# A retention and gated-MLP kernel on one core: the table that sets the order of its first two batches is written anew

## The chip, the cores and the metric

The kernel runs on one core of one Trainium2 chip. The metric is the device time of one execution in microseconds (us), the median of three runs. TensorE (PE) multiplies, VectorE (DVE), ScalarE (ACT) and GpSimd (POOL) work on its results and prepare its operands, and SyncE (SP) issues every DMA. Each engine runs its own instructions in the order in which the program lists them, and waits on semaphores for what other engines or DMAs produce.

## The reference

There are 8 batches of 576 tokens. Retention over 8 heads of 64 columns gives x; a gated MLP follows, in which one half of the hidden columns is normalised and multiplied over tokens by a matrix that all batches share.

```python
scores = scale * np.matmul(q, k.transpose(0, 1, 3, 2))
Dmat = np.where(rel >= 0, gamma[:, None, None] ** rel[None, :, :], 0.0)
x = np.matmul(scores * Dmat, v)             # 8 x 576 x (8 * 64)
h = np.maximum(x @ w_in, 0.0)               # 512 -> 1024
u, v = h[..., :512], h[..., 512:]
v_n = (v - mean(v)) / np.sqrt(var(v) + 1e-06)
v_s = np.einsum('ts,bsd->btd', w_spatial, v_n) + b_spatial[None, :, None]
out = (u * v_s) @ w_out                     # 512 -> 512
```

## The kernel before

Retention goes in chunks of 128 tokens, four to a batch, and a tail of 64. Of a chunk, `load` fetches three or one blocks (qk, kn, vv); PE makes the scores (`r<-qk`) and the state's update (`r<-vv,kn`), which needs kn scaled; DVE masks the scores (`at`); ACT or DVE adds the update to the decayed state (`sh` after 64 tokens, `st` after 128); and a burst of PE multiplies the queries with the state and the masked scores with the values (`r<-qsc,sh`, `r<-qsc,st`, `r<-at,vv`). ACT and DVE take the burst's result out in two parts of a number (`slot`, high and low). These products are 64x64 and come in blocks of 16 instructions, each of which the trace shows as two.

The MLP's products have 128 rows and 288, 256 or 512 columns. A number stands as a rounded high part and a low part, so that each product is three. The weights come as 64-bit numbers and are taken apart on the chip: `weight` makes of one block the steps `f` or `lent_vn` (sign), `m<-raw` or `m<-lent_slot` (ACT), two shifts on DVE, the high part (`win`, `wout`, on ACT) and the low part. `split_chain` turns the gated product into high and low parts in `slot`, which `f_chain`, the last product of batch 0, reads (`m<-slot,wout`).

The order of all this is written out. `ORDER` is a text of 714 steps for batches 0 and 1 and the first steps of batch 2; `STEADY` repeats for batches 2 to 5, and `LAST` ends the kernel. `run` takes the names one after the other and lets the chain of that name do its next step; `next(chain)` issues the step's instructions, and every instruction is kept in this order on its engine. So one table sets five queues at once. A name is a kind and its numbers: `d.1.0` issues the loads of batch 1, chunk 0, one a step; `D.2.1` those of a weight block (2 is `w_out`, 0 is `w_u`); `w.0.1.vp` takes one apart; `g`, `p` and `b` are scores, state and burst of a chunk; `k` scales kn; `v` is the normalised half; `V`, `G` and `P` are the spatial product, the gate and the split of batch 0; `F.0.0.3` is its last product, half 0, block 3. `z.N.1` is one idle multiplication of 512 columns (`m<-wsp`) that nobody reads: 43 of them stand in the table. `BANKS` gives each accumulation its PSUM bank, in the order of use.

```python
    def run(order, b=0):
        ...
            chain = chains.get(name)
            if chain is None:
                chain = chains[name] = makers[head](*rest)
            next(chain)
```

The buffer `raw` holds two weight blocks side by side; `fetch(2, 1)`, which is `D.2.1`, writes the half that `D.0.1` filled before and that the second shift of `w.0.1` reads.

Of the kernel before, what the change touches and what calls it, by code (L numbers as in the profile page):

```python
# [40 lines left out]


ORDER = """
    d.0.0 m z.41.1 z.34.1 d.0.0 c.a d.0.0 k.0.0.v q.0.0.p z.33.1 z.37.1 z.1.1 z.12.1 z.18.1 z.25.1 z.15.1 z.10.1
# [4 lines left out]
    w.1.2.pp b.0.1 p.0.1.aa w.1.2.pp b.0.1 b.0.1 z.20.1 v.0.0 z.27.1 z.17.1 z.39.1 z.22.1 w.1.1.vp b.0.1 p.0.1.aa
    b.0.1 v.0.1 w.1.2.pp w.1.2.pp k.0.2.a g.0.2 p.0.2.aa w.1.2.pp w.1.1.vp w.1.3.vp w.1.2.pp v.0.0 z.42.1 v.0.1  # L50
    z.36.1 v.0.0 v.0.0 v.0.1 v.0.1 D.0.2 D.0.1 d.0.3 w.0.2.pp q.0.2.p p.0.1.aa w.0.2.pp p.0.2.aa g.0.2 p.0.2.aa
    p.0.2.aa w.0.2.pp w.0.1.vp w.0.1.vp w.0.1.vp w.0.2.pp w.0.1.vp T.0 S d.1.0 S d.1.0 d.1.0 c.t D.0.0 S d.1.1
    d.1.1 d.1.1 t.0.p q.0.3.p k.1.0.p k.0.3.a b.0.2 g.0.3 b.0.2 v.0.0 t.0.p b.0.2 b.0.2 p.0.3.ap p.0.2.aa b.0.2
    v.0.0 b.0.2 p.0.3.ap v.0.1 v.0.0 v.0.0 t.0.p g.0.3 v.0.1 z.26.1 z.29.1 z.11.1 z.5.1 v.0.2 v.0.2 v.0.2 z.9.1
    v.0.2 z.23.1 z.24.1 z.14.1 v.0.0 p.0.3.ap p.0.3.ap w.0.0.vp b.0.3 s.2.p v.0.1 b.0.3 g.1.0 v.0.0 w.0.0.vp v.0.2
    g.1.0 w.0.0.vp b.0.3 b.0.3 p.1.0.pp g.1.1 e.0.v e.0.v e.0.v w.0.0.vp v.0.1 v.0.4 v.0.4 v.0.4 z.16.1 z.35.1
    s.1.p b.0.3 w.0.2.pp p.1.0.pp w.0.0.vp v.0.1 b.0.3 v.0.3 v.0.3 v.0.4 v.0.3 v.0.3 q.1.0.p s.2.p k.1.1.p s.1.p
    p.1.0.pp w.0.0.vp d.1.2 S S v.0.2 w.0.1.vp v.0.2 v.0.2 s.3.p v.0.2 v.0.4 v.0.1 v.0.2 U.0 U.1 b.1.0 v.0.4 s.5.p
    v.0.4 v.0.3 s.0.p p.1.0.pp v.0.4 p.1.1.pp v.0.4 b.1.0 U.1 v.0.3 U.0 v.0.3 s.4.p g.1.1 v.0.3 v.0.3 v.0.4 v.0.3
    v.0.4 b.1.0 b.1.0 D.2.1 d.1.2 T.1 D.2.0 D.2.2 d.1.2 s.3.p w.0.2.pp q.1.1.p d.1.3 d.1.3 d.1.3 D.0.3 s.0.p G.1.2  # L60
    q.1.2.p p.1.0.pp s.5.p s.4.p v.0.4 v.0.4 p.1.1.pp p.1.1.pp p.1.1.pp w.0.1.vp k.1.2.p p.1.1.pp w.0.3.pv V.0.0
    V.0.0 V.0.0 V.0.0 V.0.3 V.0.0 V.1.0 b.1.0 V.0.0 b.1.0 V.0.3 w.2.1.vp w.2.1.vp V.1.0 w.2.1.vp V.1.2 V.0.2
    w.2.1.vp w.2.0.vv V.1.2 w.2.0.vv b.1.1 p.1.2.pa w.2.1.vp b.1.1 w.0.3.pv w.2.0.vv G.1.2 w.2.0.vv w.0.3.pv
    w.0.3.pv g.1.2 b.1.1 b.1.1 w.0.3.pv V.0.2 V.1.1 G.0.2 v.1.0 D.2.3 d.2.0 d.2.0 A.0.5.v A.0.0.v w.0.3.pv g.1.2
    p.1.2.pa w.2.2.vv G.0.3 V.1.1 w.2.0.vv p.1.2.pa p.1.2.pa G.0.2 q.1.3.p A.0.1.p k.1.3.p w.2.2.vv G.0.3 A.0.2.v
    A.0.6.v t.1.p V.0.1 G.0.1 p.1.2.pa V.0.1 b.1.1 b.1.1 w.2.0.vv v.1.0 A.0.9.v A.0.12.v w.2.2.vv p.1.3.pp b.1.2
    b.1.2 A.0.3 A.0.7 A.0.13.v A.0.14 P.0.1.p w.2.2.vv G.0.1 g.1.3 t.1.p b.1.2 b.1.2 v.1.0 V.1.3 v.1.0 G.1.3 v.1.1
    v.1.1 v.1.1 v.1.1 A.0.15.v p.1.3.pp w.2.3.vp p.1.3.pp w.2.1.vp d.2.1 d.2.0 d.2.1 b.1.2 t.1.p g.1.3 b.1.2 V.1.3
    A.1.5.p v.1.0 w.2.3.vp G.1.3 w.2.3.vp w.2.3.vp p.1.3.pp k.2.0.v v.1.0 b.1.3 b.1.3 p.2.0.vp b.1.3 g.2.0 b.1.3
    G.1.1 e.1.v P.0.0.p v.1.0 e.1.v e.1.v v.1.0 G.1.1 P.0.0.p P.0.1.p v.1.4 v.1.4 v.1.4 y.1.2.0 v.1.4 p.2.0.vp  # L70
    v.1.1 v.1.1 w.2.3.vp v.1.0 v.1.1 v.1.0 b.1.3 w.2.2.vv y.1.2.0 v.1.4 A.0.10 P.1.0.v y.1.1.0 y.1.1.0 A.0.4.v
    A.1.1.v w.2.2.vv v.1.1 v.1.1 v.1.1 g.2.0 p.2.0.vp y.1.0.0 F.0.0.0 y.1.0.0 F.0.0.0 P.1.1.v A.0.11.v A.0.8.v
    P.1.1.v b.1.3 v.1.4 F.0.0.2 v.1.2 v.1.2 F.0.0.1 v.1.2 v.1.2 v.1.4 w.2.3.vp F.0.0.1 F.0.0.2 v.1.2 A.1.0.v
    p.2.0.vp p.2.0.vp A.1.2.p A.1.3 P.1.0.v F.0.1.0 F.0.0.0 F.0.0.1 A.1.6.v A.1.9.v v.1.2 A.1.12.p v.1.4 A.1.13.v
    A.1.7 F.0.1.0 F.0.1.1 v.1.2 F.0.1.1 F.0.0.3 F.0.0.3 v.1.4 v.1.4 v.1.4 v.1.4 v.1.2 v.1.4 q.2.0.v F.0.0.3 F.0.1.0
    F.0.1.1 F.0.0.2 F.0.1.3 F.0.1.3 A.1.14 v.1.3 v.1.3 v.1.3 v.1.3 F.0.1.2 g.2.1 b.2.0 v.1.3 v.1.3 v.1.3 F.0.1.2
    v.1.3 b.2.0 v.1.3 y.1.3.1 y.1.2.1 y.1.3.1 k.2.1.a y.1.2.1 y.1.1.1 A.2.1.v A.1.4.p A.2.5.v A.1.15.p A.2.0.p
    A.2.2.v A.2.6.v v.1.3 A.2.9.v A.1.8.v A.2.12.v y.1.1.1 A.2.7 v.1.2 b.2.0 b.2.0 T.2 d.2.1 p.2.1.vv d.2.2 d.2.2
    d.2.2 F.0.1.3 y.1.3.0 g.2.1 v.1.2 X.1.1.2 X.1.1.2 A.2.3 A.2.10 A.1.10 b.2.0 X.1.0.0 X.1.0.1 y.1.0.1 q.2.1.v
    t.2.v A.2.11.v p.2.1.vv y.1.3.0 A.2.8.v b.2.1 b.2.1 p.2.1.vv p.2.1.vv k.2.2.v p.2.1.vv A.1.11.v X.1.0.1 X.1.0.0  # L80
    A.2.13.v A.2.14 y.1.0.1 A.2.15.v g.2.2 b.2.1 p.2.2.vv b.2.1 d.2.3 d.2.3 d.2.3 X.1.1.3 X.1.1.0 X.1.1.1 g.2.2
    A.2.4.v p.2.2.vv X.1.1.3 p.2.2.vv p.2.2.vv X.1.1.0 b.2.1 Y.1.3.p Y.1.1.v k.2.3.v Y.1.1.v X.1.1.1 Z.1.5.vv
    X.1.0.2 q.2.2.p b.2.2 b.2.2 Y.1.3.p Z.1.7.vv p.2.2.vv X.1.0.2 Z.1.6.vv p.2.3.vp t.2.v b.2.2 g.2.3 b.2.2
    W.1.2.0.A X.1.0.3 W.1.2.1.A Z.1.7.vv b.2.2 Z.1.6.vv W.1.2.0.A Z.1.5.vv p.2.3.vp q.2.3.v d.3.0 d.3.0 F.0.1.2
    t.2.v p.2.3.vp g.2.3 p.2.3.vp Z.1.6.vv Z.1.7.vv X.1.0.3 b.2.3 b.2.3 Y.1.2.v Z.1.5.vv k.3.0.v Y.1.2.v g.3.0
    b.2.3 b.2.3 e.2.p W.1.2.1.A W.1.2.0.A Z.1.4.vv e.2.p W.1.2.0.A Z.1.4.vv e.2.p R.2.1.v W.1.2.0.C W.1.2.0.B
    Z.1.4.vv W.1.2.0.C W.1.2.0.A W.1.2.1.A W.1.2.1.B W.1.2.0.A b.2.3 W.1.2.1.A R.2.3.v W.1.2.1.A W.1.2.1.C
    W.1.2.1.A R.2.2.p R.2.1.v K.2.5.vp W.1.2.0.B W.1.2.0.C d.3.1 d.3.0 W.1.2.0.B R.2.3.v W.1.2.1.C W.1.2.1.E
# [962 lines left out]
```

## Time and profile before

| | |
|---|---|
| median of 3 runs | 503.67 us (502.77, 503.67, 505.89) |
| the profiled execution's own time | 504.22 us |
| its span, first to last instruction | 502.4 us |
| PE busy | 495.2 us of the span |
| DVE, ACT, POOL busy | 391.3, 259.4, 154.1 us |
| moved by DMA | 55.53 MB |

The time of an execution is its span and 1.8 us around it. Busy PE is not PE at its peak, since multiplications overlap: what counts is when the next one begins.

### The profile page before, as it was taken

Reading aid. Unit: us, or ns where it says so; the run is one execution under the profiler, and the core shown is the slowest. Engines: PE = TensorE matmul, PEld = TensorE weight load, DVE = VectorE, ACT = ScalarE, POOL = GpSimd, SP = SyncE. Lnnn points to the kernel's source line nnn. Section 1 sums busy time; section 2 is a strip of 40 time slices with the busy share of each in tenths; the row PEclk is TensorE's granted clock in tenths of the full one; section 3 lists DMA queues with packets and bytes.
Section 4 is the critical chain, followed back from the end, with each engine's and each line's share of the span. In section 5 each row is a group of like instructions: output and inputs, shape, how many; then the busy total and the mean of one; then the engine's idle time right before and its main releaser. Section 6 shows DMA issues by size and latency. Waiting matters only on the chain.

```text
span 502.4 us, 17010 instructions
## 1 busy us (share of the span) xinstructions
PE 495.2 (99%) x7335; PEld 472.8 (94%) x7335; DVE 391.3 (78%) x869; ACT 259.4 (52%) x587; POOL 154.1 (31%) x133
## 2 busy tenths in 40 slices
...
GB/s 303 418 271 316 77 146 24 24 102 97 98 142 164 162 86 2 87 208 123 50 10 156 136 168 0 44 168 165 91 2 64 225 94 3 1 48 48 2 1 94
DMA packets 26429, 55.53 MB, mean 111 GB/s; under 512 B 2929, under 2 KB 11249, under 8 KB 26098
## 3 DMA queue, kind: packets, MB, share of 16 engines
...
q14 instruction: 18, 0.15, 0.1%
...
## 4 chain that ended last, share of the span: by engine, by line
PE 94%; DVE 2%; ACT 1%; DMA 1%; issue 1%; POOL 0%; SPq 0%; ACTq 0%
PE m L203 79%; PE r L203 14%; DMA vv<-in_qkv 1%; ACT places L203 0%; DVE x L203 0%; POOL x L203 0%; DVE u L203 0%; DVE lent_vn L203 0%; DVE m L203 0%; ACT slot L203 0%; SPq L203 0%; DVE o L203 0%; DVE xt L203 0%; ACT xt L203 0%; DVE places L203 0%
## 5 line engine op out<-in xcount | busy, mean ns | idle before, releaser
L203 PE MATMUL m<-wsp,vn 128*128 128x288 f32 x768 | 112.7, 296 | 0.0
L203 PEld LDWEIGHTS m<-wsp,vn 128*128 128x128 f32 x768 | 105.0, 188 | 0.6
L203 DVE TENSOR_TENSOR u<-m,u 128x288 f32<-128x288 f32 (+1 forms) x132 | 57.1, 438 | 23.2 <-PE m L203 11.9
L203 ACT COPY u<-m 128x288 f32<-128x288 f32 (+1 forms) x92 | 34.8, 386 | 40.8 <-PE m L203 33.4
L203 PE MATMUL m<-slot,win 128*128 128x288 f32 x336 | 49.8, 296 | 0.0
L203 PEld LDWEIGHTS m<-slot,win 128*128 128x128 f32 x336 | 46.3, 188 | 0.9 <-ACT vn L203 0.2
L203 ACT CAST slot<-u 128x576 fp32r<-128x576 f32 x32 | 21.5, 675 | 45.3 <-DVE u L203 44.6
L203 DVE SCALAR_TENSOR_TENSOR u<-u,m 128x288 f32<-128x288 f32 x48 | 21.3, 451 | 26.6 <-PE m L203 26.4
L203 PE MATMUL m<-slot,wout 128*128 128x288 f32 x264 | 37.5, 294 | 0.0
L203 PEld LDWEIGHTS m<-slot,wout 128*128 128x128 f32 x264 | 36.0, 188 | 0.2
L203 PE MATMUL m<-win,slot 128*128 128x512 f32 (+1 forms) x168 | 36.2, 349 | 0.0
L203 ACT CAST places<-u 128x576 fp32r<-128x576 f32 x21 | 14.2, 675 | 39.0 <-DVE u L203 39.0
L203 POOL TENSOR_TENSOR dec<-st,fixed_terms 128x256 f32<-128x256 f32 x16 | 14.3, 895 | 64.6 <-DVE st L203 64.6
L203 POOL TENSOR_TENSOR qk<-qk,fixed_terms 128x512 f32<-128x512 f32 (+1 forms) x16 | 21.9, 1369 | 35.3 <-PE r L203 29.9
L203 PEld LDWEIGHTS m<-win,slot 128*128 128x128 f32 x168 | 26.7, 188 | 4.2 <-DVE slot L203 0.5
L203 PE MATMUL m<-quarter,slot 128*128 128x256 f32 x216 | 28.9, 281 | 0.1
L203 POOL TENSOR_TENSOR slot<-u,slot 128x576 fp32r<-128x576 f32 x7 | 10.0, 1436 | 59.5 <-ACT slot L203 53.9
L203 PEld LDWEIGHTS m<-quarter,slot 128*128 128x128 f32 x216 | 27.1, 188 | 0.7 <-ACT u L203 0.3
L203 PE MATMUL m<-wtl,vt 128*128 128x288 f32 (+1 forms) x128 | 27.2, 295 | 0.0
L203 PE MATMUL m<-places,wout 128*128 128x288 f32 x168 | 26.3, 297 | 0.0
L203 PE MATMUL m<-slot,part 128*128 128x288 f32 x168 | 25.3, 298 | 0.0
L203 DVE TENSOR_TENSOR at<-r,fixed_terms 128x512 f32<-128x512 f32 x32 | 21.9, 683 | 3.9 <-PE r L203 2.0
...
## 6 DMA issues: line engine op xcount, KB each, us to landing
qk<-in_qkv SPq DMA_DIRECT2D x30, 512.0 KB, 4.0
...
lent_slot<-in_w_v SPq DMA_DIRECT2D x4, 512.0 KB, 8.4
raw<-in_w_u SPq DMA_DIRECT2D x4, 512.0 KB, 10.8
```

The costliest lines, as they stand in the source:

```text
L203: ins = op(*args, **kw)
```

## The change

`ORDER` and `BANKS` are written anew. The 714 steps are the same ones, each as often as before, the 43 idle multiplications among them, on the same engines; only their order and the banks differ. `STEADY`, `LAST` and every function are unchanged.

```diff
 ORDER = """
-    d.0.0 m z.41.1 z.34.1 d.0.0 c.a d.0.0 k.0.0.v q.0.0.p z.33.1 z.37.1 z.1.1 z.12.1 z.18.1 z.25.1 z.15.1 z.10.1
-    z.3.1 z.4.1 z.28.1 g.0.0 p.0.0.va z.31.1 z.7.1 p.0.0.va b.0.0 z.8.1 D.1.0 D.1.3 g.0.0 w.1.0.vp p.0.0.va
+    c.a d.0.0 d.0.0 k.0.0.v q.0.0.p m d.0.0 z.26.1 z.13.1 z.29.1 z.2.1 z.21.1 z.34.1 z.32.1 z.4.1 z.14.1 z.16.1
+    z.28.1 z.22.1 g.0.0 p.0.0.va z.40.1 z.0.1 z.39.1 p.0.0.va b.0.0 D.1.0 p.0.0.va p.0.0.va g.0.0 w.1.0.vp w.1.0.vp
...
```

The first place is the start. On DVE before, the mask of chunk 0 (`at_161`) stands ahead of the first state, and the low part of the burst's result (`slot_189`) ahead of the shifts for the first weight blocks; `sh`, which the burst of chunk 1 needs, is the last row here.

```order
L203 TENSOR_TENSOR kn_95<-kn_95,fixed_terms 128x512
L203 TENSOR_TENSOR at_161<-r_91,fixed_terms 128x512
L203 TENSOR_SCALAR lent_vn_92<-lent_slot_93 128x512
L203 TENSOR_TENSOR dec_79<-sh,fixed_terms 128x256
L203 TENSOR_TENSOR st_76<-r_91,dec_79 128x256
...
L203 TENSOR_TENSOR slot_189<-r_90,slot_189 128x2x4x64
L203 SCALAR_TENSOR_TENSOR m_87<-m_87,lent_vn_92 128x512
L203 SCALAR_TENSOR_TENSOR lent_vn_92<-lent_slot_93,m_87 128x512
L203 SCALAR_TENSOR_TENSOR m_86<-m_86,lent_vn_92 128x512
L203 SCALAR_TENSOR_TENSOR lent_vn_92<-lent_slot_93,m_86 128x512
L203 TENSOR_TENSOR sh<-r_91,dec_78 128x256
```

DVE now, the same stretch.

```order
L203 TENSOR_TENSOR kn_96<-kn_96,fixed_terms 128x512
L203 TENSOR_TENSOR dec_79<-sh,fixed_terms 128x256
L203 TENSOR_TENSOR st_76<-r_91,dec_79 128x256
L203 TENSOR_TENSOR at_161<-r_91,fixed_terms 128x512
L203 TENSOR_SCALAR lent_vn_92<-lent_slot_93 128x512 x2
L203 SCALAR_TENSOR_TENSOR m_89<-m_89,lent_vn_92 128x512
L203 SCALAR_TENSOR_TENSOR lent_vn_92<-lent_slot_93,m_89 128x512
L203 SCALAR_TENSOR_TENSOR m_87<-m_87,lent_vn_92 128x512
L203 SCALAR_TENSOR_TENSOR lent_vn_92<-lent_slot_93,m_87 128x512
L203 TENSOR_TENSOR slot_197<-r_90,slot_197 128x2x4x64
L203 TENSOR_SCALAR lent_vn_92<-lent_slot_93 128x512
L203 TENSOR_TENSOR sh<-r_91,dec_78 128x256
```

The state of chunk 0 now comes ahead of its mask, and `sh` of chunk 1 stands behind one more instruction, the sign step of the third weight block (`TENSOR_SCALAR lent_vn`), which before stood right behind it.

ACT a little later, before: the rows that stand ahead of the scaling of chunk 2's kn (`u<-u`, eight instructions), which the update of chunk 2 on PE needs.

```order
L203 ACTIVATE dec_79<-sh,fixed_terms 128x64 x4
L203 ACTIVATE m_86<-lent_slot_93 128x512
L203 CAST win_66<-lent_vn_92 128x512
L203 CAST slot_189<-r_90 128x2x4x64
L203 ACTIVATE u<-u,fixed_terms 128x64 x8
```

ACT now.

```order
L203 ACTIVATE dec_79<-sh,fixed_terms 128x64 x4
L203 CAST win_66<-lent_vn_92 128x512
L203 CAST slot_197<-r_90 128x2x4x64
L203 ACTIVATE m_87<-lent_slot_93 128x512
L203 ACTIVATE u<-u,fixed_terms 128x64 x8
```

A step of the fourth weight block (`m<-lent_slot`) moved from ahead of the two casts to behind them.

The second place is SP's queue between the first loads and batch 1. Before, qk of batch 1, chunk 0 (`qk_94`) is issued behind one row of the spatial matrix (`in_w_sp`), and its kn and vv (`kn_95`, `vv_417`) soon after; the first `w_out` block comes later, after the rows shown.

```order
L203 DMA tail<-in_tails 128x768
L203 DMA lent_slot_93<-in_w_sp 128x576
L203 DMA qk_94<-in_qkv 128x1024
L203 DMA lent_slot_93<-in_w_sp 128x576
L203 DMA kn_95<-in_qkv 128x512
L203 DMA vv_417<-in_qkv 128x512
L203 DMA amt<-in_tmask 128x256
L203 DMA raw<-in_w_u 128x512
```

SP now, from the same tail on.

```order
L203 DMA tail<-in_tails 128x768
L203 DMA qk_199<-in_qkv 128x1024
L203 DMA kn_200<-in_qkv 128x512
L203 DMA raw<-in_w_out 128x512
L203 DMA raw<-in_w_u 128x512
L203 DMA amt<-in_tmask 128x256
L203 DMA qk_95<-in_qkv 128x1024
L203 DMA lent_slot_93<-in_w_sp 128x576
L203 DMA kn_96<-in_qkv 128x512
L203 DMA vv_432<-in_qkv 128x512
```

Two blocks of chunk 1 (`qk_199`, `kn_200`) and two weight blocks, the first of which is `D.2.1`, now go ahead of the blocks of chunk 0 (`qk_95`, `kn_96`, `vv_432`).

The third place is the first product of batch 0 with `w_out`, some 80 us into the program. On PE before, the burst of batch 1's last chunk (`att,tail` is its end) is followed by products of `win` with `slot` and with `xt`; the first `m<-slot,wout` comes 40 rows later.

```order
L203 MATMUL r_90<-at_266,vv_417 64x64 x16
L203 MATMUL r_90<-att,tail 64x64 x8
L203 MATMUL m_88<-slot_189,win_66 128x288 x2
L203 MATMUL m_88<-slot_189,win_67 128x288
...
L203 MATMUL m_87<-win_66,xt 128x512
L203 MATMUL m_87<-win_67,xt 128x512
```

PE now.

```order
L203 MATMUL r_90<-at_261,vv_432 64x64 x16
L203 MATMUL r_90<-att,tail 64x64 x8
L203 MATMUL r_91<-vv_201,kn_96 64x64 x16
L203 MATMUL m_86<-slot_197,wout_1095 128x288 x2
L203 MATMUL m_86<-slot_197,wout_1098 128x288
...
L203 MATMUL m_89<-slot_197,win_66 128x288 x2
L203 MATMUL m_89<-slot_197,win_67 128x288
```

`F.0.0.3`, the last of its four blocks before, now is the first, and stands right behind the burst and one update. The two instructions of POOL that make the low parts for it (`slot<-u,slot`, two steps `P`) keep their place among POOL's rows.

## Rows read from the trace of the kernel before

**Rows 1.** Windows: length, busy PE, PEld, DVE, ACT, POOL, PEclk, DMA, GB/s.
```profile
8.00:21.30 13.30, 12.30 (x297) 9.19 (x297) 10.34 (x19) 9.85 (x29) 7.71 (x7) 1.00 1.03 419
21.30:45.30 24.00, 23.94 (x428) 19.94 (x426) 19.78 (x47) 22.05 (x59) 17.66 (x16) 1.00 0.86 317
45.30:160.00 114.70, 114.70 (x1732) 109.52 (x1733) 94.14 (x185) 60.06 (x136) 44.84 (x38) 1.00 0.33 103
160.00:176.90 16.90, 16.50 (x419) 15.80 (x422) 14.10 (x40) 10.05 (x25) 7.91 (x8) 1.00 0.46 148
```

**Rows 2.** Timeline of PE to 45: start, length, what, [idle before, releaser].
```profile
8.05 0.69 PE L203 MATMUL r<-vv,kn 64*64 64x64 f32 x32 [0.33 <-DMA vv<-in_qkv]
...
15.62 0.24 PE L203 MATMUL r<-qsc,sh 64*64 64x64 f32 x1 [0.57 <-DVE sh L203]
...
16.46 0.27 PE L203 MATMUL r<-qsc,st 64*64 64x64 f32 x1 [0.38 <-ACT r L203]
...
17.32 0.50 PE L203 MATMUL m<-wsp 128*128 128x512 f32 x1
...
18.36 1.09 PE L203 MATMUL m<-wsp 128*128 128x512 f32 x4
19.28 0.96 PE L203 MATMUL m<-win,slot 128*128 128x512 f32 x3
20.17 1.16 PE L203 MATMUL r<-u 64*64 64x64 f32 x64
21.26 0.96 PE L203 MATMUL m<-win,slot 128*128 128x512 f32 x3
```

**Rows 3.** Timeline of PE, 168.8 to 171.
```profile
170.01 0.44 PE L203 MATMUL r<-vv,kn 64*64 64x64 f32 x10 [0.40 <-issue]
```

**Rows 4.** Timeline of DVE, 8 to 36.
```profile
15.05 0.42 DVE L203 TENSOR_TENSOR sh<-r,dec 128x256 f32<-128x256 f32 x1
15.39 0.42 DVE L203 TENSOR_SCALAR lent_vn<-lent_slot 128x512 int32<-128x512 int32 x1
15.72 0.68 DVE L203 TENSOR_TENSOR at<-r,fixed_terms 128x512 f32<-128x512 f32 x1
...
17.10 0.69 DVE L203 SCALAR_TENSOR_TENSOR lent_vn<-lent_slot,m 128x512 int32<-128x512 int32 x1
...
26.80 1.28 DVE L203 SCALAR_TENSOR_TENSOR f<-raw,m 128x512 int32<-128x512 int32 x2
```

**Rows 5.** Timeline of ACT, 8 to 36.
```profile
17.32 0.61 ACT L203 ACTIVATE m<-lent_slot 128x512 f32<-128x512 f32 x1
17.88 0.60 ACT L203 CAST win<-lent_vn 128x512 fp32r<-128x512 f32 x1
18.39 0.57 ACT L203 CAST slot<-r 128x512 fp32r<-128x512 f32 x1
18.87 2.02 ACT L203 ACTIVATE u<-u,fixed_terms 128x64 f32<-128x64 f32 x8
```

**Rows 6.** DMA issues of window 15.6 to 16.0: count, KB, us to landing.
```profile
qk<-in_qkv SPq DMA_DIRECT2D x1, 512.0 KB, 10.9
```

**Rows 7.** Timeline of POOL, 0 to 46.
```profile
27.98 1.04 POOL L203 TENSOR_TENSOR kn<-kn,fixed_terms 128x512 f32<-128x512 f32 x1
```

**Rows 8.** Timeline of PE, 33.3 to 37.
```profile
35.41 0.68 PE L203 MATMUL r<-vv,kn 64*64 64x64 f32 x32
35.88 0.68 PE L203 MATMUL r<-qk 64*64 64x64 f32 x32
```

**Rows 9.** Timeline of POOL, 70 to 110.
```profile
83.83 2.88 POOL L203 TENSOR_TENSOR slot<-u,slot 128x576 fp32r<-128x576 f32 x2 [5.53 <-DVE slot L203]
```

**Rows 10.** Timeline of PE, 62 to 112.
```profile
80.07 0.27 PE L203 MATMUL r<-qsc,sh 64*64 64x64 f32 x1
...
82.61 1.86 PE L203 MATMUL m<-slot,win 128*128 128x288 f32 x12
...
90.90 3.33 PE L203 MATMUL m<-slot,wout 128*128 128x288 f32 x24
```

More of the change, by code (lines that the diff above doesn't have):

```diff
@@ L49 @@
[L49 to L88, printed above, removed]
@@ L89 @@
-    W.1.2.0.B W.1.2.0.E q.3.0.p K.2.7.pv R.2.2.p W.1.2.1.B K.2.6.vp W.1.2.0.E K.2.4.vp W.1.2.0.B W.1.2.1.C d.3.1
-    W.1.2.0.B d.3.1 W.1.2.1.B W.1.2.1.B p.3.0.pv K.2.5.vp K.2.7.pv K.2.7.pv K.2.6.vp p.3.0.pv p.3.0.pv W.1.2.1.E
-    W.1.2.1.B K.2.6.vp W.1.2.0.E W.1.2.1.E p.3.0.pv W.1.2.1.B K.2.4.vp g.3.0 p.3.0.pv K.2.5.vp K.2.4.vp
+    c.a d.0.0 d.0.0 k.0.0.v q.0.0.p m d.0.0 z.26.1 z.13.1 z.29.1 z.2.1 z.21.1 z.34.1 z.32.1 z.4.1 z.14.1 z.16.1
+    z.28.1 z.22.1 g.0.0 p.0.0.va z.40.1 z.0.1 z.39.1 p.0.0.va b.0.0 D.1.0 p.0.0.va p.0.0.va g.0.0 w.1.0.vp w.1.0.vp
@@ new lines @@
+    b.0.0 z.15.1 D.1.3 b.0.0 b.0.0 w.1.3.vp w.1.0.vp w.1.3.vp z.31.1 z.12.1 z.10.1 z.19.1 z.17.1 z.27.1 b.0.0 d.0.1
+    d.0.1 d.0.1 k.0.1.p q.0.1.p g.0.1 p.0.1.aa z.37.1 z.1.1 z.38.1 z.20.1 z.33.1 z.7.1 z.30.1 w.1.0.vp w.1.3.vp
+    w.1.3.vp b.0.0 D.1.1 D.1.2 w.1.1.vp d.0.2 p.0.0.va p.0.1.aa g.0.1 b.0.1 w.1.3.vp w.1.0.vp w.1.1.vp w.1.1.vp
+    w.1.1.vp b.0.1 p.0.1.aa w.1.0.vp w.1.2.pp w.1.1.vp z.36.1 z.8.1 b.0.1 b.0.1 b.0.1 p.0.1.aa b.0.1 z.18.1 v.0.0
+    z.6.1 v.0.1 w.1.2.pp w.1.2.pp w.1.2.pp k.0.2.a g.0.2 p.0.2.aa w.1.1.vp w.1.3.vp w.1.2.pp w.1.2.pp q.0.2.p
@@ new lines @@
+    z.41.1 z.11.1 z.35.1 v.0.0 v.0.1 v.0.1 v.0.0 v.0.1 v.0.0 D.0.1 d.0.3 D.0.2 S S T.0 w.0.2.pp p.0.1.aa w.0.1.vp
+    w.0.1.vp p.0.2.aa w.0.1.vp g.0.2 p.0.2.aa p.0.2.aa w.0.1.vp w.0.2.pp k.0.3.a d.1.1 d.1.1 D.2.1 D.0.0 c.t d.1.0
+    S d.1.0 d.1.0 b.0.2 p.0.3.ap g.0.3 s.1.p b.0.2 q.0.3.p k.1.1.p t.0.p s.1.p t.0.p b.0.2 b.0.2 q.1.0.p k.1.0.p
+    v.0.0 p.0.2.aa b.0.2 w.0.2.pp w.0.2.pp v.0.0 g.0.3 z.25.1 z.24.1 z.9.1 z.3.1 z.23.1 b.0.2 v.0.1 v.0.0 v.0.0
+    p.0.3.ap v.0.2 v.0.2 v.0.2 z.42.1 z.5.1 v.0.2 t.0.p v.0.1 p.0.3.ap v.0.0 p.0.3.ap s.0.p w.0.2.pp v.0.0 b.0.3
@@ new lines @@
+    w.0.0.vp b.0.3 g.1.0 g.1.0 b.0.3 b.0.3 g.1.1 p.1.0.pp w.0.0.vp s.2.p w.0.0.vp e.0.v e.0.v e.0.v w.0.0.vp v.0.4
+    v.0.4 v.0.4 v.0.4 v.0.2 v.0.1 v.0.1 b.0.3 w.0.0.vp p.1.0.pp b.0.3 v.0.3 v.0.3 v.0.3 v.0.3 v.0.1 w.0.1.vp v.0.2
+    v.0.1 v.0.2 v.0.4 v.0.2 v.0.2 v.0.4 w.0.0.vp v.0.2 U.0 U.1 b.1.0 s.0.p p.1.0.pp s.2.p q.1.1.p p.1.0.pp p.1.0.pp
+    w.0.2.pp T.1 S d.1.1 S v.0.4 v.0.3 v.0.3 v.0.4 p.1.1.pp s.3.p U.0 s.4.p s.3.p D.2.2 d.1.2 d.1.3 v.0.3 b.1.0
+    b.1.0 b.1.0 v.0.4 U.1 s.5.p v.0.3 p.1.1.pp v.0.4 v.0.3 s.4.p s.5.p w.0.1.vp G.1.2 V.0.0 v.0.3 b.1.0 V.0.0 V.0.0
@@ new lines @@
+    v.0.4 v.0.4 v.0.4 V.0.3 V.0.0 V.0.3 V.1.2 V.1.2 g.1.1 b.1.0 G.1.2 V.0.0 V.1.0 D.2.0 w.2.0.vv w.2.0.vv V.1.0
+    w.2.0.vv V.0.0 D.0.3 d.1.2 d.1.3 k.1.3.p p.1.1.pp q.1.2.p p.1.1.pp d.1.3 d.1.2 w.2.0.vv w.2.1.vp k.1.2.p
+    p.1.1.pp w.0.3.pv V.0.2 b.1.1 b.1.1 g.1.2 b.1.1 b.1.1 p.1.2.pa w.0.3.pv V.0.2 V.0.1 G.0.1 b.1.1 b.1.1 w.0.3.pv
+    g.1.2 w.0.3.pv V.1.1 V.0.1 w.2.1.vp w.0.3.pv w.0.3.pv G.0.1 w.2.1.vp w.2.1.vp A.0.0.v p.1.2.pa t.1.p p.1.2.pa
+    q.1.3.p A.0.1.p v.1.1 v.1.1 v.1.1 w.2.0.vv w.2.1.vp w.2.1.vp w.2.0.vv D.2.3 w.2.3.vp w.2.3.vp v.1.1 v.1.0 v.1.1
```

31 lines of the change are left out of this document (27 added, 4 removed).

## The prediction

> **What bounds the kernel now.** I read the windows first, since the change touches one stretch: the table's steps run from the start to some 177 us, and everything behind them keeps its order. In that stretch PE is the engine that is never free. From 45.3 to 160 us it is busy for 114.70 of 114.70 us, from 21.3 to 45.3 for 23.94 of 24.00, while DVE, the next, has 94.14 of 114.70 [rows 1]. A new order can't shorten PE's work, for the list of steps is the same; it can only take away waits of PE or add some. So the second reading is PE's timeline at the start, the only place where it waits. DMA fills that place: its share is 1.03 from 8.0 to 21.3 us, at 419 GB/s [rows 1].
>
> PE's waits there are four. The first update of a state begins at 8.05, when vv lands. The burst of chunk 1 waits 0.57 us for `sh` from DVE and, half way, 0.38 for ACT [rows 2]. Behind them come idle multiplications, from 17.32 on, that wait for nothing and cost 0.23 us each (four of them take PE from 18.36 to 19.28) [rows 2]. That is the hidden reserve: the 43 idle multiplications are time on PE whether it has a wait to fill or not. Last, one gap of 0.40 us in the middle of a block of updates near 170 us, for which no semaphore is named [rows 3]. The three gaps together are 1.35 us; with them gone the kernel would be 0.3% faster. Anything below about 1% (5 us) can hardly be told from no change here, as the runs before lie 3 us apart.
>
> **The start, worked out.** Until the data land, nothing differs: the terms, qk, kn and vv of chunk 0 are loaded in another order, but vv is the fourth in both, so the first update stays at 8.05 [rows 2], and 12 idle multiplications in place of 13 ahead of it cost or save nothing.
>
> Then the burst of chunk 1. On DVE the same instructions stand ahead of `sh` as before and one more, the sign step of the third weight block, which ran right behind it. The two change places, so `sh` comes one spacing later: 15.39 in place of 15.05, a shift of 0.34 [rows 4]; if that weight block lands late, some tenths more. I take 0.44. The burst's first half goes from 15.62 to 16.06. Its second half had waited for ACT until 16.46; now two idle multiplications lie between the halves, and the masked scores come from DVE behind `sh` as before (`at`, 15.72 before, 16.16 now, 0.68 long) [rows 4], so the values can start at 16.9 to 17.1. The burst is over, and the next idle multiplication starts, at about 17.8, against 17.32 [rows 2]: 0.48 later. But the changed order has by then spent 31 of the 43 idle multiplications, the old one 26 (I counted the z steps on PE's row). Five of them, 1.15 us, have moved into time in which PE would have waited. Balance here: 0.48 - 1.15 = -0.67 us.
>
> The next wait takes most of it back. The update of chunk 2 (the second half of the 64 `r<-u` at 20.17 [rows 2]) needs kn scaled by eight ACT instructions that ran from 18.87 to 20.89 [rows 5]. Before, ACT did one weight step at 17.32 ahead of the two casts; now it does it behind them, right ahead of the scaling, and the first cast needs a DVE shift that ran from 17.10 to 17.79 [rows 4]. On DVE the same instructions stand ahead of that shift in both orders, only turned among themselves, so I move its end by no more than 0.1, to 17.87. ACT's chain is then: cast 17.9, second cast 18.4, weight step 18.9, scaling from 19.5 (spacings of 0.51, 0.48 and 0.56 between such rows [rows 5]), end 21.5 to 21.6. The update's last part ends at 21.75, and the next product starts at 21.9 in place of 21.26 [rows 2]: 0.64 later. Up to here 33 idle multiplications are spent against 31, which gives back 0.46. Balance: **+0.2 us**, and it replaces the -0.67, as both are counted from the start. The bounds: if the weight step doesn't delay the scaling (0.6), the balance is -0.4; if the third block lands so late that `sh` loses 0.5 more, +0.7.
>
> **The loads of batch 1.** Before, qk of chunk 0 of batch 1 was issued at about 15.7 and landed 10.9 us later, at 26.6 [rows 6], and kn was scaled at 27.98 for an update at 35.41 [rows 7, 8]: a cover of over 6 us. Now two blocks of 512 KB and two small ones go ahead on SP's queue, and the first (`D.2.1`) waits until DVE has done the second shift of the block that lies in its place. That shift is the second of the pair that began at 26.80 and ended at 28.08 before [rows 4]; in the new order it stands ahead of the pair's other half, so I put it between 25.9 and 28.1. From there to kn's landing lie 512, 512, 128, 512, 288 and 256 KB, 2.26 MB, which is 5.4 us at 419 GB/s [rows 1]. DMA is full until about 27.9 with what goes ahead, so kn lands at about 33.3, is scaled by 34.4 (1.04 [rows 7]), and the update, which now stands behind the scores of the next chunk (0.47, from 35.41 to 35.88 [rows 8]) and two more idle multiplications, comes at 36.5. Cost: nothing, with 2 us of cover left. If the shift ends at 28.1 rather than 25.9 and nothing else fills DMA until then, those 2.2 us come on top, and PE waits 0.2, with tenths of DMA's spread 0.5 us. I take 0.
>
> **The rest.** From 45 to 160 us PE has no wait to lose [rows 1], so a new order can only cost there. The place with the least cover that I found is the first product with `w_out`. Before, POOL made the low parts for it from 83.83 to 86.71 [rows 9], and PE came to it at 90.90 [rows 10], 4.2 us later. Now it stands where PE is at about 82.7: right behind the burst and one update, which ended at 82.61 [rows 10]. ACT's second cast for it stands behind the copy of a product that PE ends before the 12 products and the burst ahead of `F.0.0.3`: 12 times 0.14 (24 take 3.33), and 80.07 to 82.61 [rows 10], 4.2 us together. In them must fit three ACT instructions of 0.6 [rows 5] and one of POOL, half of 2.88 [rows 9]: 3.2 us. The cover is 1.0 us. Cost: 0, and from there one for one. All other moves I take together at nothing, since PE's row between 90 and 160 us has the same blocks in nearly the same lengths, and DVE, ACT and POOL have the same work with 18% and more to spare [rows 1].
>
> **The gap near 170 us.** I leave its 0.40 us in. The profile shows that PE stood still inside a block of 32 updates with 10 of them left, and names no releaser [rows 3]; that it was a load of instructions is likely and not shown. If it is gone, -0.4.
>
> The Trainium skill (Runtime: NRT & Kernel Launch, section Instruction fetch mechanics) says that each engine fetches its instructions itself in blocks of 256 ahead of use, and that the cost of a block's edge is mostly hidden. By that rule an order made for late loads of instructions would gain nothing anywhere, and the 0.40 us would stay. The trace agrees as far as 45 to 160 us go, where PE has no idle time, and the row near 170 us speaks against it.
>
> **The sum.** 504.22 of the profiled execution + 0.2 + 0 + 0 = 504.4. That execution was 0.55 over the median, so the median comes to 503.67 + 0.2 = **503.9**, which is no change. Its own range is 502.7 to 505.2: the start's bounds (-0.4, +0.7), the loads' 0.5 and the spread of single runs.
>
> **Rivals.** *Slower: `F.0.0.3` comes too early.* If DVE or ACT is behind at 78 us by more than the 1.0 us of cover, PE waits for the low parts. The upper bound is that POOL ends them when it did before, at 86.71: PE then waits 86.7 - 82.7 = 4.0 us. Time 505 to 507.9; the middle is 506. For it speaks that DVE is the busiest engine behind PE there, against it that POOL's own row is unchanged and it waited 5.53 us for DVE's part before [rows 9], so POOL has room. It decides from the moment that the second cast begins later than about 80.7.
>
> *Faster: the waits go and don't come back.* The scaling isn't delayed, the five idle multiplications stay hidden, and the gap near 170 us goes: -0.67 - 0.4 - 0.3 (tenths that PE waits for single rows between 21.3 and 36; 0.06 of them are in [rows 1]) = -1.4, which gives 502.3. More isn't there: the idle time of PE from 8 to 177 us is 1.46 us [rows 1].
>
> *The change doesn't do what it says.* If loads of instructions never held an engine in this stretch but for that gap, the order is simply another one of the same worth. That gives the forecast's time again, 503.9, and can't be told from it by the time.
>
> **Chances.** Forecast with the third rival 0.64; slower through an early `F.0.0.3` or a like wait 0.20; faster 0.16. A gain over 1% would need 5 us and PE has 1.46 to give: 0.02. A loss over 1% needs the slow rival at its end and a second wait beside it: 0.07. Within 1%: 0.91. The range for 8 in 10 goes from 501.6 to 507.2: from a little below the fast rival's 502.3 to most of the slow one's.
>
> **What would show it.** In the profile after, DVE's `sh` near 15.5; the idle multiplication behind the burst of chunk 1 near 17.8; ACT's eight scalings starting near 19.5 and the next `m<-win,slot` near 21.9; qk of batch 1 landing at 32 rather than 26.6 with no wait of PE at 36; `m<-slot,wout` first at 82.8 without idle time ahead of it; and a PE that is busy all through 45 to 160 us. I am wrong if PE waits there for DVE, ACT or POOL, or if the first update is no longer at 8.05.

## The result, and the profile after

The changed kernel takes 507.25 us (median of 9 runs) against 503.62 for the kernel before (9 runs): a ratio of means of 1.0069, interval 1.0051 to 1.0087. It is 3.6 us slower, under 1%, at the very end of the range (507.2); the forecast of 503.9 missed what costs it. One of the nine, the execution that was profiled first, ran at a granted clock of 0.56 from about 8 us to its end (790 us); the ratio leaves it out, and the median without it is 507.15. The lines below are from two later executions of the same kernel: *first* (508.39 us, its own time) and *second* (506.51).

The windows of the table's stretch, first execution, which answer to [rows 1] (length, busy PE, PEld, DVE, ACT, POOL, PEclk, DMA, GB/s):

```profile
8.00:21.30 13.30, 13.29 (x280) 9.40 (x272) 10.77 (x20) 10.15 (x29) 7.69 (x6) 1.00 1.02 417
21.30:45.30 24.00, 23.52 (x423) 19.66 (x420) 19.39 (x47) 22.09 (x59) 16.68 (x15) 1.00 0.80 281
45.30:160.00 114.70, 112.59 (x1702) 107.57 (x1702) 87.57 (x179) 57.83 (x131) 42.09 (x35) 0.99 0.32 102
160.00:176.90 16.90, 16.90 (x340) 16.32 (x340) 14.59 (x36) 9.06 (x21) 11.36 (x11) 1.00 0.57 188
```

The start has become better: PE's idle time between 8 and 21.3 us went from 1.00 to 0.01. But PE now waits 0.48 us in the second row, and at its end the two kernels are level: PE has begun 763 multiplications by 45.20 us before and 763 by 45.28 now. The damage is in the third row, where PE had been busy for 114.70 us and now is for 112.59, at a clock of 0.99. All 2.1 us are one wait, in none of the three places that were shown ahead of the prediction. It is what the timeline of all engines from 47 to 55 us shows (first execution; start, length, what, idle time before and releaser):

```profile
48.13 2.94 POOL L203 TENSOR_TENSOR wtl<-lent_slot,wtl 1x576 fp32r<-1x576 f32 x2
...
48.63 2.94 PE L203 MATMUL m<-wsp,vn 128*128 128x288 f32 x21
...
51.11 0.59 ACT L203 CAST slot<-r 128x512 fp32r<-128x512 f32 x1 [2.83 <-POOL wtl L203]
51.59 1.26 ACT L203 ACTIVATE vt<-m,sm 64x512 fp32r<-64x512 f32 x2
52.88 0.74 DVE L203 SCALAR_TENSOR_TENSOR vt<-m,sm,vt 64x512 fp32r<-64x512 f32 x1 [3.82 <-ACT vt L203]
...
53.68 0.53 PE L203 MATMUL m<-wtl,vt 128*128 128x288 f32 x2 [2.10 <-DVE vt L203]
```

The same stretch of the kernel before, in lines not shown yet:

```profile
48.48 2.92 POOL L203 TENSOR_TENSOR wtl<-lent_slot,wtl 64x576 fp32r<-64x576 f32 x2
48.55 1.26 ACT L203 ACTIVATE vt<-m,sm 64x512 fp32r<-64x512 f32 x2
...
49.84 0.75 DVE L203 SCALAR_TENSOR_TENSOR vt<-m,sm,vt 64x512 fp32r<-64x512 f32 x1 [0.42 <-ACT vt L203]
...
51.44 0.59 ACT L203 CAST slot<-r 128x512 fp32r<-128x512 f32 x1 [1.64 <-POOL wtl L203]
...
51.65 0.70 PE L203 MATMUL m<-wtl,vt 128*128 128x288 f32 x4
```

ACT's copy of batch 1's first burst (`slot<-r`, the fifth step of `b.1.0`) waits for POOL in both, and POOL is no later now (it ends its rows `wtl` at 51.07, before at 51.40). The copy writes `slot` of batch 1, the buffer in which the rows of the spatial matrix lie until POOL has made the last low parts of `wtl`. Before, that wait of 1.64 us held nobody: the two instructions that make `vt` stood ahead of the copy. In the new table the last three steps of `v.0.4` stand behind it, so `vt` is held until POOL is done, DVE's part follows ACT's, and the spatial product on PE, which needs `vt` for its last two multiplications, stands still.

Behind the wait the clock fell. The windows of the first execution, and of the second, in the same columns:

```profile
53.70:55.00 1.30, 1.30 (x9) 1.30 (x10) 1.24 (x2) 0.40 (x1) 1.30 (x2) 0.96 0.05 19
55.00:58.40 3.40, 3.40 (x16) 3.40 (x16) 0.32 (x1) 0.72 (x2) 2.39 (x3) 0.51 0.00 0
58.40:62.00 3.60, 3.60 (x31) 3.44 (x34) 2.31 (x7) 0.32 (x1) 0.01 (x1) 1.00 0.00 0
```
```profile
53.60:55.00 1.40, 1.36 (x10) 1.36 (x11) 1.29 (x2) 0.40 (x1) 1.23 (x2) 1.00 0.04 15
55.00:58.40 3.40, 3.40 (x28) 3.40 (x27) 1.04 (x2) 1.04 (x2) 2.64 (x3) 1.00 0.00 0
```

After a pause of 2.10 us PE ran at 0.51 (1.2 GHz) for the 3.4 us of the second row and did 16 multiplications there; after one of 2.06 us, in another execution of the same program, it stayed at full speed and did 28. The two executions were level ahead of the pause (48.63 and 48.64); the part of the spatial product that begins at 59.96 in the first begins at 58.39 in the second, 1.57 us sooner. The pause is in both; the fall of the clock is not.

### The profile page after: what moved, and what is told of

It reads as the page before. It is cut to its first block, busy times and chain, and to the rows that moved or that the text cites. A ratio compares the mean times of both kernels' runs of the same rounds, so it can differ in the third digit from the quotient of the medians.

```text
span 788.8 us, 17019 instructions
## 1 busy us (share of the span) xinstructions
PE 783.9 (99%) x7335; PEld 700.1 (89%) x7335; DVE 392.1 (50%) x869; ACT 259.6 (33%) x587; POOL 148.2 (19%) x133
## 4 chain that ended last, share of the span: by engine, by line
PE 99%; DVE 0%; issue 0%; ACT 0%
PE m L203 85%; PE r L203 14%; DVE wsp L203 0%; DVE o L203 0%; ACT r L203 0%; DVE warm L203 0%; DVE eps L203 0%
## 5 line engine op out<-in xcount | busy, mean ns | idle before, releaser
L203 PE MATMUL m<-wsp,vn 128*128 128x288 f32 x768 | 177.9, 406 | 0.0
L203 PEld LDWEIGHTS m<-wsp,vn 128*128 128x128 f32 x768 | 153.4, 222 | 13.1
L203 PE MATMUL m<-slot,win 128*128 128x288 f32 x336 | 77.9, 402 | 0.0
L203 PEld LDWEIGHTS m<-slot,win 128*128 128x128 f32 x336 | 66.7, 216 | 7.4 <-issue 1.6
L203 PE MATMUL m<-slot,wout 128*128 128x288 f32 x264 | 59.7, 391 | 0.0
L203 PE MATMUL m<-win,slot 128*128 128x512 f32 (+1 forms) x168 | 55.3, 488 | 0.0
L203 PEld LDWEIGHTS m<-quarter,slot 128*128 128x128 f32 x216 | 43.7, 273 | 1.1
L203 PEld LDWEIGHTS m<-places,wout 128*128 128x128 f32 x168 | 34.2, 229 | 2.4 <-issue 0.2
L203 PEld LDWEIGHTS m<-slot,part 128*128 128x128 f32 x168 | 33.1, 234 | 2.6
L203 PE MATMUL m<-slot,quarter 128*128 128x288 f32 x144 | 35.1, 413 | 0.0
```

The lines of the kernel that those rows point to most:

```text
L203: ins = op(*args, **kw)
```

## The experiments

**The changed kernel again,** without an edit.

> The changed kernel once more, unedited, for a profile at full clock: the execution that was profiled first ran at a granted clock of 0.56 from 8 us on and took 790 us, so it says nothing of where 3.6 us went. Theory (an early wait that isn't made good, or a wait for the low parts ahead of the first product with w_out): span about 505, with one place between 15 and 85 us at which PE falls 3 to 4 us behind the kernel before. Rival (scattered losses in the table's middle): span about 505, with no single gap over 0.5 us and the difference growing a little at a time between 45 and 177 us.

> The changed kernel, unedited, for more executions with their granted clock. Theory (PE's wait for vt is always there, 2.1 to 2.3 us, and the fall of the clock behind it in some executions only, for 1.5): executions with a mean clock of 0.999 or 1.0 take 506.0 to 506.8, those with 0.995 to 0.997 take 506.8 to 508.6, and between the means of the two lie 1.0 to 1.6 us. Rival (the clock has no part in it): the two groups lie within 0.4.

The first gave the lines above: one place, as theory had it, though not a place that the forecast had named. The second gave 506.71 us (5 runs, ratio 1.0070, 1.0058 to 1.0082). Of the other 14 executions of this kernel, six have a mean granted clock of 0.999 or more and take 506.51 to 506.85; eight have 0.995 to 0.997 and take 506.77 to 508.53. The means, 506.6 and 507.8, lie 1.1 us apart: executions with the low clock cost 1.1 on average, and are 8 of 14. Where the clock fell is seen in one of the eight, the first execution; that it is the same place in the other seven is taken from their mean clock and not shown.

**The copy behind `vt`, and the reverse in the kernel before.**

```diff
 (the changed kernel)
-... V.0.0 v.0.3 b.1.0 V.0.0 V.0.0 v.0.4 v.0.4 v.0.4 V.0.3 ...
+... V.0.0 v.0.3 V.0.0 V.0.0 v.0.4 v.0.4 v.0.4 b.1.0 V.0.3 ...
 (the kernel before: the fifth b.1.0 and the last three v.0.4 go, in this order, ahead of the fourth V.0.0)
```

> The changed kernel with one step moved: b.1.0's fifth, ACT's copy of the burst into slot, goes behind the three steps v.0.4 that make vt. Theory (that copy waits until POOL has read the spatial matrix out of the same buffer, and holds vt up behind it): PE's wait of 2.1 us before the first product with vt is under 0.2, the granted clock stays at full speed behind it, the time falls by 3.3 to 3.8 to about 504, within 0.15% of the kernel before. Rival (vt is late for another reason, the kn and terms of POOL or DVE's own queue): less than 1 us is gained. Rival (the loss is spread over the table): 506 or more.

> The kernel before with the same step moved the other way: ACT's copy into slot ahead of the last three steps v.0.4. Theory: POOL ends its reading at about 51.4 as before, vt comes at about 54.0 in place of 50.6, PE waits 2.2 to 2.4 us and then runs some 20 products at half clock: slower by 3.5 to 4.0 us, about 507.3. Rival (the rest of the new table is what costs): the copy ahead of vt costs under 1 us, 503.6 to 504.5.

f1 took 504.05 us (11 runs; 1.0011 of the kernel before, 1.0003 to 1.0020): from 1.0069 to 1.0011, some 2.9 of the 3.6 us, by moving one step (3.3 to 3.8 were expected). f2 took 506.03 (6 runs; 1.0058, 1.0039 to 1.0076): the copy put ahead of `vt` makes the old table, too, slower by 2.7. This took four steps, since the last three `v.0.4` stand further ahead there. Timeline of f1 and then of f2:

```profile
47.74 1.24 ACT L203 ACTIVATE vt<-m,sm 64x512 fp32r<-64x512 f32 x2
...
50.67 0.59 ACT L203 CAST slot<-r 128x512 fp32r<-128x512 f32 x1 [1.69 <-POOL wtl L203]
...
50.99 0.44 PE L203 MATMUL m<-wtl,vt 128*128 128x288 f32 x2
```
```profile
51.64 0.58 ACT L203 CAST slot<-r 128x512 fp32r<-128x512 f32 x1 [2.81 <-POOL wtl L203]
52.12 1.25 ACT L203 ACTIVATE vt<-m,sm 64x512 fp32r<-64x512 f32 x2
...
54.21 0.81 PE L203 MATMUL m<-wtl,vt 128*128 128x288 f32 x4 [2.19 <-DVE vt L203]
```

In f1 the copy still waits for POOL, and again nobody stands behind it. In f2 PE waits 2.19 us. I had expected 507.3, since I took the fall of the clock as certain: the mean clock is 0.997 in three of six executions (506.50 to 507.82), one of which was profiled (0.50 from 55.5 to 58.5 us), and the other three took 504.77 to 505.55, 2.0 us less on average.

**POOL sooner.** ACT's order stays as changed.

```diff
-... s.2.p q.1.1.p p.1.0.pp p.1.0.pp w.0.2.pp ... s.4.p s.5.p w.0.1.vp ...
+... s.2.p p.1.0.pp p.1.0.pp w.0.2.pp ... s.4.p s.5.p q.1.1.p w.0.1.vp ...
```

> The changed kernel with one step of POOL (q.1.1, the scaled queries, 1.3 us) moved behind the two low parts of the spatial matrix's last rows, which then end 1.25 us sooner, with ACT's order as in the changed kernel. Theory: PE's wait falls from 2.1 to about 0.85; the time falls by 1.25 if the half clock still follows, by 2.7 if a pause this short leaves the clock alone. Rival (POOL isn't what the copy waits for): no change.

The moved step now reads its buffer after the load of chunk 3 has overwritten it, so this kernel scales the wrong queries for chunk 1 of batch 1; the work is the same. It took 505.35 us (6 runs; 1.0035, 1.0022 to 1.0049). Timelines of POOL, ACT and PE:

```profile
47.54 2.92 POOL L203 TENSOR_TENSOR wtl<-lent_slot,wtl 1x576 fp32r<-1x576 f32 x2
...
50.50 0.59 ACT L203 CAST slot<-r 128x512 fp32r<-128x512 f32 x1 [1.69 <-POOL wtl L203]
...
53.06 0.53 PE L203 MATMUL m<-wtl,vt 128*128 128x288 f32 x2 [0.95 <-DVE vt L203]
53.44 2.14 PE L203 MATMUL m<-wsp,vn 128*128 128x288 f32 x15
```

POOL ends 0.61 us sooner than in the first execution (50.46 for 51.07), and PE reaches the spatial product 0.53 later (49.16 for 48.63), so POOL is 1.14 sooner against PE. PE's wait is 1.15 shorter: the copy waits for POOL and `vt` for the copy. All six executions have a mean clock of 0.998 to 1.0. The shorter wait and the clock that no longer falls (8/14 of 1.1, 0.65) would be 1.8 of the 1.9 us gained. That is an estimate: in this profile part of the shorter wait is PE's own delay of 0.53 us (see what f1 leaves).

**Idle multiplications in the wait**, added (f3) or moved there from 17 to 30 us (f7); `BANKS` follows the new order of use.

```diff
 (f3)
-... v.0.4 v.0.4 v.0.4 V.0.3 ...
+... v.0.4 v.0.4 v.0.4 z.43.9 V.0.3 ...
 (f7: z.18.1 z.6.1 z.41.1 z.11.1 z.35.1 z.25.1 z.24.1 z.9.1 z.3.1 in the place of z.43.9)
```

> The changed kernel with nine more idle multiplications of 512 columns (2.0 us) on PE right ahead of the products that wait for vt. They add no result. If the loss of 3.6 us is the wait of 2.1 and, apart from it, 1.4 to 1.5 us of products at half clock: the wait is filled, the clock stays at full speed, and the time falls by 1.4 to about 506.0. Rival (all of the 3.6 us is waiting, and the clock is low for some other reason than the pause): no change, 507.3, or 2 us more if the added work isn't hidden.

> The changed kernel with nine of its own 43 idle multiplications (two at 17 to 18 us, three at 21, four of those at 28) moved to right ahead of the products that wait for vt, none added. Theory: the wait is filled, the clock stays at full speed in every execution, and the nine that are missing earlier cost nothing, as in f9: 506.0 to 506.6, 0.7 to 1.3 under the changed kernel. Rival (what held f3 at 507.3 was not its nine added multiplications but something that the filling itself brings): 507.0 to 507.5.

f3 took 507.27 us (6 runs; 1.0073, 1.0061 to 1.0085), f7 506.00 (5 runs; 1.0048, 1.0035 to 1.0061). In both the clock is 0.999 or 1.0 in every execution. f3's timeline of PE:

```profile
49.20 1.34 PE L203 MATMUL m<-wsp,vn 128*128 128x288 f32 x9
50.39 2.25 PE L203 MATMUL m<-wsp 128*128 128x512 f32 x9
52.47 1.75 PE L203 MATMUL m<-wsp,vn 128*128 128x288 f32 x12
54.23 0.54 PE L203 MATMUL m<-wtl,vt 128*128 128x288 f32 x2
...
131.71 1.23 PE L203 MATMUL m<-wsp,vn 128*128 128x288 f32 x8 [0.57 <-issue]
...
232.72 0.69 PE L203 MATMUL r<-vv,kn 64*64 64x64 f32 x32 [0.64 <-issue]
...
360.46 0.40 PE L203 MATMUL m<-slot,quarter 128*128 128x288 f32 x1 [0.29 <-issue]
```

Nine idle multiplications fill the wait and PE comes out of it at full speed, in eleven of eleven executions against six of 14 without them (by the mean clock): the fall goes with the pause. What that gives back in time is not shown. f7 is 0.7 below the changed kernel beside it (506.71), as expected, but four of the five executions there had kept the full clock too (506.51 to 506.85), so the 0.7 isn't the clock's, and its cause is open. f3 missed its 506.0 and lies 0.6 over those four. Its profile, of its slowest execution (508.33), has a wait of 1.34 us for `sh` at 16.63, which neither profile of the changed kernel has and which put it 0.57 behind the first execution at the spatial product (49.20 for 48.63). It also has three gaps for which no releaser is named, 1.50 us together. The one at 232 stands where the first execution waited 0.28 for DVE; the other two are in neither profile of the changed kernel. One profile can't tell which of these belongs to the added instructions.

**What f1 leaves.** f1 was 0.7 us over the kernel before. Two profiles (f3, f4) showed DVE's sign step of the third weight block, which the new table has ahead of `sh`, at 1.5 us in place of 0.43, and PE waiting 1.34 and 1.35 us for `sh` behind it. f5 puts it behind `sh` again; f6 puts the mask ahead of it, so that it should always come when POOL is at work.

```diff
 (f5, from f1)
-... D.1.2 w.1.1.vp d.0.2 p.0.0.va p.0.1.aa g.0.1 ...
+... D.1.2 d.0.2 p.0.0.va p.0.1.aa w.1.1.vp g.0.1 ...
 (f6, from f1)
-... D.1.2 w.1.1.vp d.0.2 p.0.0.va p.0.1.aa g.0.1 ...
+... D.1.2 g.0.1 w.1.1.vp d.0.2 p.0.0.va p.0.1.aa ...
```

> The kernel of f1 (the changed one with the copy behind vt) and one more step moved: on DVE the sign step of the third weight block goes behind sh again, where it stood in the kernel before. Theory: what is left between f1 and the kernel before (0.7 us) is this step: in some executions its block lands 0.1 us later, POOL's subtraction has then begun, the step takes 1.5 us in place of 0.43, and sh and PE wait behind it (seen in two profiles of four). With the step behind sh, sh comes at about 14.4 in every execution, PE waits there under 0.2 us, and the time is 503.2 to 503.5 with a range of under 1 us: no slower than the kernel before. Rival (the 0.7 us are lost elsewhere): 504.0 as f1.

> The kernel of f1 with the mask of chunk 1 (0.68 us on DVE) moved ahead of that sign step, so that the step begins at about 14.7, when POOL's subtraction has begun in every execution. Theory: the step takes 1.2 to 1.5 us each time, sh comes at about 16.0, PE waits 1.3 us ahead of the burst, of which idle multiplications behind it don't give anything back: 0.4 to 0.9 us slower than f1, 504.5 to 505.0, and no execution under 504. Rival (the long step is a late landing, not POOL): the step takes 0.43, sh comes 0.7 later at the most, PE waits under 0.7 and the time is that of f1 within 0.3.

> The kernel of f1 once more, beside the changed kernel on one chip. Theory (the one step carries the whole loss): 3.0 to 3.6 us under the changed kernel and within 0.1% of the kernel before, so that the 0.7 us left over in the first run of f1 were the spread of executions. Rival (a second loss of 0.7 us in the new table): 504.0 again, with an interval that leaves no change out.

f5: 503.43 us (11 runs; 1.0003, 0.9994 to 1.0013). f6: 503.57 (12 runs; 0.9997, 0.9987 to 1.0008). f1 again: 504.28 (12 runs; 1.0021, 1.0008 to 1.0035), 2.4 under the changed kernel beside it. Timeline of f6 and of f5:

```profile
14.53 1.30 POOL L203 TENSOR_TENSOR win<-lent_vn,win 128x512 fp32r<-128x512 f32 x1 [0.18 <-ACT win L203]
14.56 1.54 DVE L203 TENSOR_SCALAR lent_vn<-lent_slot 128x512 int32<-128x512 int32 x1
...
16.03 0.41 DVE L203 TENSOR_TENSOR sh<-r,dec 128x256 f32<-128x256 f32 x1
...
16.59 0.24 PE L203 MATMUL r<-qsc,sh 64*64 64x64 f32 x1 [0.92 <-DVE sh L203]
```
```profile
14.21 0.41 DVE L203 TENSOR_TENSOR sh<-r,dec 128x256 f32<-128x256 f32 x1
14.54 0.42 DVE L203 TENSOR_SCALAR lent_vn<-lent_slot 128x512 int32<-128x512 int32 x1
```

The collision is as expected: begun 0.03 us after POOL's subtraction, the step takes 1.54 us and PE waits 0.92. In these two profiles it costs: PE reaches the spatial product at 48.95 in f6, at 48.37 in f5. But f6 was to take 504.5 to 505.0 and its median is that of f5. The theory foretold f5 rightly (503.2 to 503.5) and f6 wrongly; it is neither shown nor excluded, because the profile of f6 is of its slowest execution (504.25), DVE came only 0.03 us behind POOL there, and how many of the twelve have the collision isn't known. In h2 the rival came out: f1's 0.7 to 0.9 us (by medians) are there again, though f5 and f6, each one step away, don't have them. Both profiles of f1 are of executions below its median (503.55 and 503.30), and can't show them. It stays open where they are lost. That h2 lies only 2.4 under the changed kernel fits the clock, which was low in one of five executions there.

**Fewer idle multiplications.** From f5, without the 12 behind the burst of chunk 1, which stand at five places of the table (`BANKS` follows).

```diff
-    z.18.1 z.6.1 z.41.1 z.11.1 z.35.1 z.25.1 z.24.1 z.9.1 z.3.1 z.23.1 z.42.1 z.5.1
```

> The kernel of f5 without the 12 idle multiplications that stand behind the burst of chunk 1 (two at 17 to 18 us, three at 21, five and two at 28 to 33). They give no result. Theory of the forecast (idle multiplications cost PE 0.23 each whether a wait is there or not): where no wait takes their place the time falls, at most by 12 x 0.23 = 2.8 to 500.6; PE's update of chunk 0 of batch 1 already waits for kn at 36, so all that is gained ahead of it, up to 2.8, turns into that wait unless the loads move forward too: I expect a gain of 0.0 to 0.5, and a wait of 2 to 3 us at 34 to 36. Rival (loads follow PE's pace, since buffers come free sooner): 501.5 or less.

503.63 us (12 runs; 1.0006, 0.9995 to 1.0017): nothing gained. Two waits of PE's timeline, 1.45 of the 2.8 us, stand in their place:

```profile
28.83 3.32 PE L202 MATMUL m<-win,slot 128*128 128x512 f32 x12 [0.78 <-ACT slot L202]
...
33.36 0.34 PE L202 MATMUL r<-qsct,st 64*64 64x64 f32 x8 [0.67 <-DVE st L202]
```

They wait for ACT and DVE, not for kn's landing as I had put it. Against f5's profile PE is 0.4 us ahead at 140 us and 0.1 behind at 470.

**The terms first, in the kernel before.**

```diff
-    d.0.0 m z.41.1 z.34.1 d.0.0 c.a d.0.0 k.0.0.v ...
+    c.a d.0.0 m z.41.1 z.34.1 d.0.0 d.0.0 k.0.0.v ...
```

> The kernel before with one DMA moved: the decay terms are loaded ahead of qk and kn of chunk 0, as in the changed kernel. Theory (that order is why the first update came 0.54 sooner there, 7.51 for 8.05): vv lands at 7.2 to 7.4 in place of 7.91 and the first update starts at 7.4 to 7.6. What comes of it at the end is nothing, within 0.3 us, since sh of chunk 1 still comes from DVE behind two shifts and the loads go at their own pace: 503.1 to 503.6. Rival (vv's landing varies from execution to execution): 7.9 as before.

502.84 us (11 runs; 0.9986, 0.9978 to 0.9995): 0.14% faster than the kernel before, with an interval that leaves no change out, and the lowest median of all that ran. vv lands at 7.32 us, as expected (issued at 2.09). PE's first update starts at 7.79 for 8.05 [rows 2] and not at 7.4 to 7.6, since the scores ahead of it began at 7.27. DMA issues of the first 3 us (KB, us from issue to landing):

```profile
fixed_terms<-in_terms SPq DMA_DIRECT2D x1, 390.0 KB, 3.2
...
vv<-in_qkv SPq DMA_DIRECT2D x1, 256.0 KB, 5.2
```

In the kernel before these were 5.1 and 5.8. That one execution lands vv sooner by chance, the rival, doesn't fit the other profiles: vv took 4.9 to 5.4 us in all twelve with the terms first, 5.6 and 5.8 in the two of the old order (f2 and the kernel before). That the start passes its gain on (0.57 us of the median) is what I had not expected: PE is 0.31 ahead at the burst of chunk 1 (15.31 for 15.62) and 0.58 at the spatial product (47.89 for 48.47).

## Why the prediction went as it did

**No change within 1%, and the sum 504.4.** The first held, the mechanism behind it didn't. The sum fell at the step "All other moves I take together at nothing, since PE's row between 90 and 160 us has the same blocks". It looked at PE's row alone and from 90 us on; the loss came at 51 us, from ACT's row, where one step had been moved behind an instruction that already waited 1.64 us. That term was about 2.9 us (f1), not 0: 2.1 of wait, and some 0.65 for the clock (1.1 in 8 of 14 executions). With the 0.7 to 0.9 that f1 leaves, whose place is open, that is the 3.6.

**"From 45 to 160 us PE has no wait to lose, so a new order can only cost there"** was right, and is the reason why the range reached far upward. The slow rival had the kind right (a wait of PE for an operand that comes too late) and the place wrong. That the time lies near the upper end of its 505 to 507.9 is luck, since that range was worked out for `F.0.0.3`, and there PE didn't wait. POOL's and PE's lines of the first execution, from two timelines:

```profile
84.19 1.92 POOL L203 TENSOR_TENSOR slot<-u,slot 128x576 fp32r<-128x576 f32 x1 [1.08 <-ACT slot L203]
```
```profile
86.67 1.58 PE L203 MATMUL m<-slot,wout 128*128 128x288 f32 x10
```

POOL ended at 86.11, PE came at 86.67: 0.56 us of cover were left of the 1.0, as this step of POOL took 1.92 us where the forecast had half of 2.88.

**The start, +0.2.** The step "vv is the fourth in both, so the first update stays at 8.05" failed: it came at 7.51 (and at 7.67 in the second execution), since the order of the three loads ahead of vv counts (f8). From there all is sooner than forecast: `sh` at 14.84 for 15.49 (15.39 and the 0.1 I added), the idle multiplication behind the burst at 17.32 for 17.8, ACT's scaling at 18.95 for 19.5. The update of chunk 2 ended at 21.29, with 33 idle multiplications spent, against 21.26 with 31: the balance is 0.03 - 0.46 = -0.43 in place of +0.2. It lies at the lower bound of -0.4, and the loads of batch 1 took it back.

**The idle multiplications as a reserve.** "Time on PE whether it has a wait to fill or not" is refuted as a credit by f9: with 12 fewer the time didn't fall, and waits for ACT and DVE stood in their place. At the start PE isn't the only bound.

**The loads of batch 1** cost 0 by the forecast, up to 0.5 by its bound. PE's timeline, first execution:

```profile
34.27 0.70 PE L203 MATMUL r<-qk 64*64 64x64 f32 x32 [0.23 <-DMA qk<-in_qkv]
...
36.72 0.69 PE L203 MATMUL r<-vv,kn 64*64 64x64 f32 x32 [0.24 <-POOL kn L203]
```

Both waits are 0.47 us together (in the second execution one of 0.20): the cover of 2 us was gone. `D.2.1` went out at 25.28, even sooner than forecast, but kn, issued at 28.14, took 7.4 us and landed at 35.5 in place of 33.3. The step that failed is "5.4 us at 419 GB/s": from 30 to 35.6 us the DMA engines moved 279 GB/s.

**The gap near 170 us** is in neither profile of the changed kernel, nor in f8 or f2, which have the old order there; f2 has one of 0.26 us at 28 and f3 has three elsewhere. So it goes with an execution rather than with the order; what such gaps are is not shown. By the Trainium skill (Runtime: NRT & Kernel Launch, section Instruction fetch mechanics) the cost of a block's edge in the fetch of instructions is mostly hidden. Ten of the twelve profiles of the experiments name no such gap on PE (f2 and f3 do), so for most executions the trace agrees.
